# An attention and feed-forward kernel: the planner that orders its instructions makes eight passes with deadlines, and the Softplus of four banks is planned as two operations of two

## The chip, the cores and the metric

The kernel runs on one core of a Trainium2 chip. A core has several engines that work side by side, each on its own queue of instructions, in the order in which the program lists them: TensorE (PE, matrix products; PEld is its weight load), VectorE (DVE), ScalarE (ACT), GpSimd (POOL), and SyncE (SP), which here issues all DMAs. An instruction waits until the semaphores of what it needs have been raised, and everything behind it on the same engine waits with it. The metric is the device time of one execution in microseconds (us), as the median of several runs.

## The reference

What is computed, cut to what matters (float32; the feed-forward weights arrive as float64):

```python
# attention: B=8, H=8, S=576, D=64, keys and values averaged over groups of 8
k_p = k.reshape(B, H, 72, 8, D).mean(axis=3)
v_p = v.reshape(B, H, 72, 8, D).mean(axis=3)
attn = softmax(1/sqrt(D) * q @ k_p.transpose(0, 1, 3, 2))
x = (attn @ v_p).transpose(0, 2, 1, 3).reshape(4608, 512)
# feed-forward: 512 -> 2048 -> 512
h = x @ w_in
g = h * erf(log(1 + exp(h)))
return g @ w_out
```

## The kernel before

**Tiling.** The 4608 tokens are cut into nine chunks of 512, with tokens along the free axis and features on the 128 partitions. Attention goes block by block (at most 256 tokens of one batch, `job`, lines 456 to 638): loads of keys and values that DVE sums over groups of eight (`ks<-raw`, `vs<-v`, line 470), scores on PE (`att<-kbd,q`, line 520), a maximum, a subtraction, an exponential by way of Sigmoid and a sum, a transpose on PE (lines 572 and 575), and the product with the values (lines 615 and 616), whose result is copied out of PSUM as a part of `x`. Each factor of a large product is split into a high and a low part (`halves`, lines 340, 341 and 352), and three matmuls of 512 columns stand for one product (`three`, line 687).

**Stages.** Chunk 0 is done plainly: `plain_in` (16 first-layer tiles in groups of four) and `second` (the second layer). The weights are unpacked from float64 on the way (lines 386 to 399), used, and stored to HBM for later (lines 409, 412, 420, 422). Chunks 1 to 8 go in four pairs. For each pair the first layer is a scheme of seven products instead of eight (`sides`, `head`, `quad`: eight quads of four output tiles each). Some of its weights are sums of weight blocks, called `ws` (`sums`, line 430 to 444); the first pair makes them on the fly. The second layer of the first pair is plain, that of the other pairs again takes seven products (`seconds`). The activation of each group of four tiles (`activation`, line 689) is Softplus on four banks of PSUM or four tiles (`d<-h` or `d<-g`, line 697), Erf on the two 1024-wide halves (`d<-d`, line 701), and a multiplication with `h` on DVE or POOL (`g<-d,h`, line 708, and `g<-d,g`, line 705). Softplus and Erf (which shares a table set with the Sigmoid of the attention) need different tables on ACT, so a table load stands where the kind changes.

**What sets the order.** None of this is written in the order in which it runs. Every call of `op` (line 143) notes an operation: its engine or two engines to choose from, a cost in ns, a priority `prio` (a due time written out by hand, in units of some 5 us), and the buffers that it reads and writes. `order` (line 182) is a list scheduler: it keeps the time at which each engine is free, looks at the operations that are ready, and on each engine picks the one with the least start time plus 30 ns (400 ns on SP) for each unit of `prio`; then it takes the earliest of the engines' picks. Buffers are places: there are 87 places of 2 KB for all large tiles, eight banks of PSUM, and a limit for each kind of tile (`CAPS`, line 52; `h` may hold 6 banks). An operation whose first touch of a tile finds no free place starts when one comes free. `WINDOW` keeps an operation from running more than 10 units ahead. A change of the ACT tables is planned at 1300 ns. Before the first large product PE is kept busy with filler matmuls on constants (`h<-cst`, line 937); the planner puts in as many as its idle time there holds (line 246).

Of the kernel before, what the change touches and what calls it, by code (L numbers as in the profile page):

```python
# [13 lines left out]
AF = mybir.ActivationFunctionType  # L14
# [7 lines left out]
SP = S // POOL  # L22
# [14 lines left out]


WINDOW = 10
T0, T0_STEP = -10.5, 1.5  # L40
VAL_R = 3.5
KEYS, KEYS_R, KEYS_S = -5.5, 0.5, -1.0
# [13 lines left out]
DGE = 1200  # L56
# [71 lines left out]
class Program:  # L128
# [14 lines left out]
    def op(self, eng, cost, prio, fn, reads=(), writes=(), hold=(), alt=None, funcs=None, port=False, turn=None):  # L143


        o = Op(eng, cost, prio, fn)
        o.set, o.port = funcs, port
        o.choice = {eng: (cost, fn)}
        if alt:
            o.choice[alt[0]] = alt[1:]  # L150
        o.bufs.extend(hold)
        deps = {}
        for accesses, write in ((reads, False), (writes, True)):
            for a in accesses:
                buf, key = a if isinstance(a, tuple) else (a, None)
                if isinstance(buf, Buf) and buf not in o.bufs:
                    o.bufs.append(buf)
                for k, (writer, readers) in buf.state.items():
                    if key is None or k is None or k == key:
                        for d in ([writer] if writer else []) + (readers if write else []):  # L160
                            if d is not o:
                                deps[d] = deps.get(d, False) or d is writer
                if write:
                    if key is None:
                        buf.state.clear()
                    buf.state[key] = (o, [])
                else:
                    buf.state.setdefault(key, (None, []))[1].append(o)
        for b in o.bufs:
            b.left += 1  # L170
        for d, flow in deps.items():
            d.next.append((o, flow))
            o.wait += 1
        if turn is not None:
            if turn in self.turns:
                self.turns[turn].follow.append(o)
                o.wait += 1
            self.turns[turn] = o
        self.ops.append(o)
        return o  # L180

    def order(self):
        free = {e: 0.0 for e in self.DELAY}
        free["SP"] = 2150.0
        port = 0.0
        slots = {t: [(0.0, i) for i in range(n)] for t, n in self.capacity.items()}
        avail = {e: [] for e in free}
        for i, o in enumerate(self.ops):
            o.key = (o.prio, i)
# [6 lines left out]
        spare = None  # L196
# [3 lines left out]
        for _ in self.ops:  # L200
# [38 lines left out]
            loaded = o.set or loaded  # L239
            if spare is not None and o.eng == "PE":  # L240
                if start > FILL:
                    heapq.heappush(slots["bank"], (start, spare[1]))
                    spare = None
                else:
                    idle = start - max(free["PE"], 3000.0) - MARGIN - (1800 if not free["PE"] else 0)
                    out.extend([self.filler] * int(idle / 107))
            end = free[o.eng] = start + o.cost
            if e == "POOL" or (e == "DVE" and o.port):
                port = end
            o.done = True  # L250
            while todo and todo[0][2].done:
                heapq.heappop(todo)
            progress = todo[0][0] if todo else progress
            for b in o.bufs:
                if not b.held:
                    b.held = True
                    b.places = {t: heapq.heappop(slots[t])[1] for t in b.limits}
                    b.place = b.places[b.home]
                b.left -= 1
                b.end = max(getattr(b, "end", 0.0), end)  # L260
                if not b.left:
                    for t in b.limits:
                        heapq.heappush(slots[t], (b.end + 150, b.places[t]))
            for d in o.follow:
                d.wait -= 1
                if not d.wait:
# [26 lines left out]
def moe_attention(ctx: ExitStack, tc: tile.TileContext, cst, qa, kl, vl, wi, wo, out):  # L293
    nc = tc.nc
# [26 lines left out]
    def act(n, psum=False):  # L321
        return 0.84 * n + (160 if psum else 190)
# [366 lines left out]
    def activation(hs, prio):  # L689

        ys = [Buf(space, [P, 2, 512], F32, "d", "d") for _ in range(2)]
        y = lambda k: ys[k // 2].ap[:, k % 2]
        own = [(ys[k // 2], k % 2) for k in range(4)]

        def softplus():
            for k, (h, _) in enumerate(hs):
                nc.scalar.activation(y(k), h.ap, AF.Softplus)  # L697

        op("ACT", 4 * act(512), prio, softplus, [h for h, _ in hs], own, funcs="softplus")
        for k in range(2):  # L700
            op("ACT", act(1024), prio + 0.2, lambda k=k: nc.scalar.activation(ys[k].ap, ys[k].ap, AF.Erf),  # L701
               own[2 * k:2 * k + 2], own[2 * k:2 * k + 2], funcs="sigmoid")
        for k, (h, g) in enumerate(hs):
            if g is h:
                both(True, dve(512), gps(512), prio + 0.3, lambda e, k=k, h=h: e.tensor_mul(  # L705
                    h.ap, y(k), h.ap), [own[k], h], [h])
            else:
                op("DVE", dve(512), prio + 0.3, lambda k=k, h=h, g=g: nc.vector.tensor_mul(  # L708
                    g.ap, y(k), h.ap), [own[k], h], [g])
# [270 lines left out]
```

## Time and profile before

| | |
|---|---|
| median of 3 runs | 883.96 us (883.89 to 884.6) |
| the profiled execution | 884.53 us |
| its span, first to last instruction | 882.5 us |
| mean granted TensorE clock in it | 0.992 |
| DVE busy | 713.5 us (81%) |
| POOL busy | 437.9 us (50%) |
| matmuls of line 687 (512 columns each) | 1584 + 1344 + 192 |
| DMA | 218.03 MB, 72.2% of what 16 DMA engines' time would hold |

A row of instructions reads: line, engine, operation, tile written `<-` tiles read, shape, count `x`; after the bar the busy time and the mean ns of one, then idle time of the engine ahead of them and what ended it. In a timeline a row begins with its start and its length in us, and the bracket at its end is the idle time ahead of it and what released it. In a table of windows each engine has its busy us in that stretch; PEclk is the granted TensorE clock, DMA the mean busy share of the DMA engines.

### The profile page before, as it was taken

The page shows a single profiled execution, that of the slowest core. Times are in us where ns is not written, and L with a number is a line of the kernel's source. Part 1 is how long each engine was busy: PE and PEld are TensorE (multiplying, and loading weights), DVE is VectorE, ACT ScalarE, POOL GpSimd, SP SyncE. Part 2 cuts the span into 40 slices and gives each one's busy share as a digit, 9 for nine tenths or more (in the row PEclk, how much of TensorE's full clock was granted, in tenths as well). Part 3 has the DMA queues.
Part 4 walks back from the last instruction along what each step waited for, and adds up shares of the span by engine and source line. Part 5 has one row for each costly group of instructions (what it writes and reads, how often), then busy time and mean ns, then how long its engine had stood idle before and what let it go on. Part 6 is the DMA issues. An engine that isn't in the chain of part 4 may idle for free. (4 is left out here: it accounts for less than half of the span.)

```text
span 882.5 us, 13579 instructions
## 1 busy us (share of the span) xinstructions
PE 852.9 (97%) x4106; PEld 701.0 (79%) x4106; DVE 713.5 (81%) x1264; ACT 561.6 (64%) x1002; POOL 437.9 (50%) x453
## 2 busy tenths in 40 slices
PE   8989899979899999999999999999999999999998
PEld 6777788768778888888887888888888888888886
DVE  5978779868888889578999998889898984567982
ACT  4778867648964475268766734587867445887630
POOL 1777578436856883035485333155474312484210
PEclk9999999989999999999999999999999999999999
DMA  8677999799898959997474367974633679448541
GB/s 286 228 243 243 295 353 321 253 375 383 294 340 315 374 196 375 353 355 268 141 267 146 119 204 262 352 238 121 227 120 120 203 268 350 118 121 266 175 163 52
DMA packets 125207, 218.03 MB, mean 247 GB/s; under 512 B 16976, under 2 KB 31440, under 8 KB 125136
## 3 DMA queue, kind: packets, MB, share of 16 engines
q1 hardware_dynamic: 125136, 217.18, 72.2%
q8 instruction: 33, 0.54, 0.3%
q14 instruction: 38, 0.31, 0.1%
HBM read 167.84 MB, written 49.28 MB: 246 GB/s over the span
## 5 line engine op out<-in xcount | busy, mean ns | idle before, releaser
L687 PE MATMUL o<-gl,w 128*128 128x512 f32 x1584 | 377.0, 393 | 1.6 <-DVE gl L352 1.4
L687 PEld LDWEIGHTS o<-gl,w 128*128 128x128 f32 x1584 | 292.7, 188 | 63.5 <-DVE gl L352 1.8
L687 PE MATMUL h<-x,w 128*128 128x512 f32 x1344 | 319.1, 394 | 7.5 <-DVE g L708 3.0
L687 PEld LDWEIGHTS h<-x,w 128*128 128x128 f32 x1344 | 250.9, 189 | 62.1 <-DVE g L708 3.2
L340 ACT ACTIVATE gl<-g 128x512 fp32r<-128x512 f32 x204 | 119.7, 624 | 74.9 <-DVE g L833 32.0
L352 POOL TENSOR_TENSOR gl<-g,gl 128x512 fp32r<-128x512 f32 x77 | 108.1, 1410 | 66.8 <-ACT gl L340 62.3
L705 POOL TENSOR_TENSOR g<-d,g 128x512 f32<-128x512 f32 x54 | 69.8, 1310 | 107.6 <-ACT d L701 93.8
L352 DVE TENSOR_TENSOR gl<-g,gl 128x512 fp32r<-128x512 f32 x139 | 107.6, 807 | 0.4 <-ACT gl L340 0.2
L770 DVE TENSOR_TENSOR g<-t,h 128x512 f32<-128x512 f32 x96 | 65.6, 684 | 41.0 <-PE h L687 39.9
L701 ACT ACTIVATE d<-d 128x1024 f32<-128x1024 f32 x72 | 72.7, 1051 | 0.3
L833 POOL TENSOR_TENSOR g<-g 128x512 f32<-128x512 f32 x48 | 67.3, 1413 | 8.8 <-DVE gl L352 6.1
L697 ACT ACTIVATE d<-g 128x512 f32<-128x512 f32 x103 | 57.5, 622 | 5.3 <-DVE g L770 5.2
L770 DVE TENSOR_TENSOR t<-t,h 128x512 f32<-128x512 f32 x57 | 39.1, 686 | 24.1 <-PE h L687 22.7
L687 PE MATMUL h<-x,ws 128*128 128x512 f32 x192 | 49.0, 410 | 6.8 <-DVE x L352 4.5
L561 POOL TENSOR_TENSOR bb<-s,z 128x64 f32<-128x64 f32 (+1 forms) x40 | 12.9, 322 | 81.1 <-DVE z L555 26.6
L687 PEld LDWEIGHTS h<-x,ws 128*128 128x128 f32 x192 | 38.1, 200 | 16.5 <-issue 6.3
L340 ACT ACTIVATE x<-xr 128x512 fp32r<-128x512 f32 (+2 forms) x64 | 34.4, 559 | 25.1 <-DVE xr L661 12.0
L615 PE MATMUL att<-et,va 128*128 128x256 f32 (+3 forms) x192 | 46.1, 340 | 1.4 <-DVE g L708 0.6
L520 PE MATMUL att<-kbd,q 128*128 128x144 f32 (+1 forms) x320 | 46.3, 287 | 1.2 <-issue 0.7
L520 PEld LDWEIGHTS att<-kbd,q 128*128 128x128 f32 (+1 forms) x320 | 42.2, 179 | 6.1 <-issue 2.2
L697 ACT ACT_TABLE_LOAD x36 | 46.2, 1283 | 0.6
L549 ACT ACTIVATE s<-s,cst 128x576 f32<-128x576 f32 (+1 forms) x36 | 27.9, 775 | 25.0 <-DVE s L545 24.8
(92 smaller groups left out, 1153.4 us busy)
## 6 DMA issues: line engine op xcount, KB each, us to landing
w<-ws SPq DMA_DIRECT2D x192, 256.0 KB, 4.8
w<-wo SPq DMA_DIRECT2D x136, 256.0 KB, 3.8
w<-wi SPq DMA_DIRECT2D x96, 256.0 KB, 5.0
ws<-ws SPq DMA_DIRECT2D x64, 256.0 KB, 5.3
v<-vl SPq DMA_DIRECT2D x48, 256.0 KB, 5.3
raw<-kl SPq DMA_DIRECT2D x32, 288.0 KB, 4.3
out<-f SPq DMA_DIRECT2D x36, 256.0 KB, 2.1
q<-qa SPq DMA_DIRECT2D x32, 256.0 KB, 5.1
```

The costliest lines, as they stand in the source:

```text
L340: op("ACT", act(n), prio, lambda: nc.scalar.activation(dst(), src(), AF.Copy, scale=scale), *access, turn=turn, alt=("POOL", 0.833 * n + 1 ...
L352: both(True, dve(n), gps(n), prio + 0.1, lambda e: e.tensor_sub(lo(), src(), f32(hi())), reads + [hikey], [lokey])
L520: nc.tensor.matmul(o, raw.ap[:, p, :T], kbd[:, p], start=(p % 2 == 0), stop=True, skip_group_check=True)
L549: op("ACT", act(H * SP) + 93, r + 0.8, lambda: nc.scalar.activation(s.ap[:T], s.ap[:T], AF.Sigmoid, bias=bias[0][:T], scale=1.0 / 64.0), [ ...
L561: nc.gpsimd.tensor_mul(bb.ap[:T], sv, zv.unsqueeze(2).broadcast_to([T, NP, 16]))
L615: nc.tensor.matmul(o, va[:, p], et.ap[:, p, :n], start=e == 0, stop=False, skip_group_check=True)
L687: nc.tensor.matmul(o, u, v, start=first and q == 0, stop=last and q == 2, skip_group_check=True)
L697: nc.scalar.activation(y(k), h.ap, AF.Softplus)
L701: op("ACT", act(1024), prio + 0.2, lambda k=k: nc.scalar.activation(ys[k].ap, ys[k].ap, AF.Erf), own[2 * k:2 * k + 2], own[2 * k:2 * k + 2 ...
L705: both(True, dve(512), gps(512), prio + 0.3, lambda e, k=k, h=h: e.tensor_mul(h.ap, y(k), h.ap), [own[k], h], [h])
L770: op("DVE", dve(512), prio, lambda: nc.vector.tensor_add(dst.ap, u.ap, o.ap), [u, o], [dst])
L833: both(True, dve(512), gps(512), prio, lambda e: e.tensor_sub(out.ap, u.ap, v.ap), [u, v], [out])
```

## The change

The planner's one run becomes the function `once`, and `order` calls it up to eight times. After each pass `latest` goes through the operations from the last to the first and works out the latest time at which each may start without making that pass longer: from the operations that need its result, from the operation that followed it on its engine, and, through the new list `after`, from the operation that took over its place in memory. These times, divided by 5100, replace `prio` in the next pass. Of all passes the one with the least planned length is kept. In the program as built all eight passes run, and the fourth is the one kept. In `activation` the Softplus of four banks, one operation until now, becomes two operations of two, which the planner may place apart. Line numbers behind 182 grow, by 59 up to `three` and by 61 from `activation` on: 470 is now 529, 687 is 746, 697 is 758, 701 is 762, 708 is 769.

```diff
@@ the planner
+PASSES, UNIT = 8, 5100.0
...
-    def order(self):
+    def reset(self):
...
+    def latest(self):
+        for o in self.ops:
+            o.late = self.length
+        for o in sorted(self.ops, key=lambda o: -o.start):
+            at = o.late - o.cost
+            for d, flow in o.next:
+                gap = self.DELAY[o.eng] if d.eng != o.eng else (self.SAME[o.eng] if flow else 0)
+                at = min(at, d.late_at - gap - o.cost)
+            for d, gap in o.after:
+                at = min(at, d.late_at - gap - o.cost)
+            o.late_at = at
+
+    def order(self, passes=PASSES):
+        best = None
+        self.prios = [o.prio for o in self.ops]
+        for n in range(passes):
+            self.reset()
+            try:
+                out = self.once()
+            except RuntimeError:
+                break
+            if best is None or self.length < best[0]:
+                best = (self.length, out, [(o.eng, o.cost, o.fn, o.start) for o in self.ops],
+                        [(b, b.place) for o in self.ops for b in o.bufs])
+            self.latest()
+            for o, p in zip(self.ops, self.prios):
+                o.prio = o.late_at / UNIT
+        self.length, out, how, places = best
...
+    def once(self):
...
+            if o.eng in last:
+                last[o.eng].after.append((o, 0))
+            last[o.eng] = o
...
-                    b.places = {t: heapq.heappop(slots[t])[1] for t in b.limits}
+                    b.places = {}
+                    for t in b.limits:
+                        _, b.places[t], by = heapq.heappop(slots[t])
+                        if by is not None and by is not o:
+                            by.after.append((o, 150 + (DGE if e == "SP" else 0)))
...
@@ the activation
-        def softplus():
-            for k, (h, _) in enumerate(hs):
-                nc.scalar.activation(y(k), h.ap, AF.Softplus)
-
-        op("ACT", 4 * act(512), prio, softplus, [h for h, _ in hs], own, funcs="softplus")
+        for i in (0, 2):
+
+            def softplus(i=i):
+                for k in (i, i + 1):
+                    nc.scalar.activation(y(k), hs[k][0].ap, AF.Softplus)
+
+            op("ACT", 2 * act(512), prio + 0.01 * i, softplus, [h for h, _ in hs[i:i + 2]], own[i:i + 2], funcs="softplus")
```

No instruction of the mathematics is added or removed. What the new order changes in kind and number: ACT holds 97 table loads instead of 73 (6 more in the stage of chunk 0, and 6, 8, 4 and 0 in the quads of the four pairs); the fillers on PE are 206 instead of 178; of the operations with a choice of engine some change sides (multiplications `g<-d,g` on POOL 68 instead of 54, high halves `gl<-g` on ACT 185 instead of 204, among others); SP issues the same 807 instructions.

**ACT, the first group of Softplus.** These are the first Softplus (`d<-h`, straight from the banks of PSUM) of chunk 0, with the Erf behind them (`d<-d`); `cv`, `low` and `w` are steps of unpacking weights. Before:

```order
L389 ACTIVATE cv<-d 128x512
L697 ACT_TABLE_LOAD
L697 ACTIVATE d<-h 128x512 x4
L389 ACTIVATE cv<-d 128x512
L701 ACT_TABLE_LOAD
L701 ACTIVATE d<-d 128x1024 x2
L340 ACTIVATE gl<-g 128x512
```

and in the changed kernel:

```order
L758 ACT_TABLE_LOAD
L758 ACTIVATE d<-h 128x512 x2
L448 ACTIVATE cv<-d 128x512
L452 ACTIVATE low<-d,cst 128x512
L762 ACT_TABLE_LOAD
L762 ACTIVATE d<-d 128x1024
L758 ACT_TABLE_LOAD
L758 ACTIVATE d<-h 128x512 x2
L448 ACTIVATE cv<-d 128x512
L762 ACT_TABLE_LOAD
L762 ACTIVATE d<-d 128x1024
```

Two banks now go through Softplus and Erf before the next two are begun, with two more table loads for the four.

**DVE, the multiplications that free those banks.** `g<-d,h` reads a bank of `h` for the last time; `vs<-v` and `ks<-raw` are sums over values and keys that come by DMA. Before:

```order
L397 SCALAR_TENSOR_TENSOR cv<-cv,low 128x512
L399 SCALAR_TENSOR_TENSOR f_934<-d,cv 128x512
L470 TENSOR_REDUCE vs<-v 128x64
L708 TENSOR_TENSOR g<-d,h 128x512 x4
L397 SCALAR_TENSOR_TENSOR cv<-cv,low 128x512 x2
```

and in the changed kernel:

```order
L458 SCALAR_TENSOR_TENSOR f_963<-d,cv 128x512
L612 TENSOR_SCALAR z<-z 64x8
L529 TENSOR_REDUCE ks<-raw 128x72
L769 TENSOR_TENSOR g<-d,h 128x512 x2
L614 RECIPROCAL z<-z 64x8
L411 TENSOR_TENSOR gl<-g,gl 128x512
L456 SCALAR_TENSOR_TENSOR cv<-cv,low 128x512
L458 SCALAR_TENSOR_TENSOR f_1039<-d,cv 128x512
L769 TENSOR_TENSOR g<-d,h 128x512 x2
```

The four multiplications stood together behind a sum over values; now they stand in two pairs, the first behind a sum over keys.

**PE, the way into the first products with `ws`.** These are the last products with the values for chunks 1 and 2 (`att<-et,va` and `att<-etb,vb`), the first-layer products with stored weights (`h<-x,w`), and the first products with sums of weights (`h<-x,ws`), which need all of `x` of both chunks. Before:

```order
L616 MATMUL att<-etb,vb 64x128
L687 MATMUL h<-x,w 128x512 x24
L615 MATMUL att<-et,va 128x128
L616 MATMUL att<-etb,vb 64x128
L615 MATMUL att<-et,va 128x128
L616 MATMUL att<-etb,vb 64x128
L687 MATMUL h<-x,ws 128x512 x18
L687 MATMUL h<-x,w 128x512 x12
```

and in the changed kernel:

```order
L675 MATMUL att<-etb,vb 64x128
L746 MATMUL o<-gl,w_2023 128x512 x2
L746 MATMUL o<-gl,w_2223 128x512
L746 MATMUL h<-x,w 128x512 x12
L674 MATMUL att<-et,va 128x128
L675 MATMUL att<-etb,vb 64x128
L674 MATMUL att<-et,va 128x128
L675 MATMUL att<-etb,vb 64x128
L746 MATMUL h<-x,ws 128x512 x18
L746 MATMUL h<-x,w 128x512 x12
```

In both the products with `ws` follow the last product with the values directly, with no other product between them.

More of the change, by code (lines that the diff above doesn't have):

```diff
@@ L180, in op @@
         return o
-    def order(self):
+    def reset(self):
+        for o in self.ops:
+            if not hasattr(o, "first"):
+                o.first = (o.wait, o.eng, o.cost, o.fn)
+            o.wait, o.eng, o.cost, o.fn = o.first
+            o.ready, o.done, o.before = 0.0, False, []
+            for b in o.bufs:
+                b.left, b.held, b.end, b.last = 0, False, 0.0, None
+        for o in self.ops:
+            for b in o.bufs:
+                b.left += 1
+    def latest(self):
+        for o in self.ops:
+            o.late = self.length
[23 more added lines that the diff above has]
+        self.length, out, how, places = best
+        for o, h in zip(self.ops, how):
+            o.eng, o.cost, o.fn, o.start = h
+        for b, p in places:
+            b.place = p
+        return out
+    def once(self):
+        for o in self.ops:
+            o.after = []
+        last, porter = {}, None
         free = {e: 0.0 for e in self.DELAY}
@@ L185, in order @@
         port = 0.0
-        slots = {t: [(0.0, i) for i in range(n)] for t, n in self.capacity.items()}
+        slots = {t: [(0.0, i, None) for i in range(n)] for t, n in self.capacity.items()}
         avail = {e: [] for e in free}
@@ L241, in order @@
                 if start > FILL:
-                    heapq.heappush(slots["bank"], (start, spare[1]))
+                    heapq.heappush(slots["bank"], (start, spare[1], None))
                     spare = None
@@ L256, in order @@
                     b.held = True
-                    b.places = {t: heapq.heappop(slots[t])[1] for t in b.limits}
+                    b.places = {}
[3 more added lines that the diff above has]
+                            by.after.append((o, 150 + (DGE if e == "SP" else 0)))
                     b.place = b.places[b.home]
                 b.left -= 1
-                b.end = max(getattr(b, "end", 0.0), end)
+                if end >= b.end:
+                    b.end, b.last = end, o
                 if not b.left:
                     for t in b.limits:
-                        heapq.heappush(slots[t], (b.end + 150, b.places[t]))
+                        heapq.heappush(slots[t], (b.end + 150, b.places[t], b.last))
             for d in o.follow:
```

## The prediction

> **What bounds the kernel now.** I read the page first, its busy shares and its slices.
>
> ```profile
> span 882.5 us, 13579 instructions
> PE 852.9 (97%) x4106; PEld 701.0 (79%) x4106; DVE 713.5 (81%) x1264; ACT 561.6 (64%) x1002; POOL 437.9 (50%) x453
> PE   8989899979899999999999999999999999999998
> L340 ACT ACTIVATE gl<-g 128x512 fp32r<-128x512 f32 x204 | 119.7, 624 | 74.9 <-DVE g L833 32.0
> L697 ACT ACT_TABLE_LOAD x36 | 46.2, 1283 | 0.6
> ```
>
> PE is the bound: from the 13th slice on (about 260 us) it is at nine tenths nearly throughout. No matmul of the mathematics goes away, so the change can only win time in which PE stands still or runs at a lower clock. Next the table of windows, for PE alone (columns: PE busy, granted clock, DMA share, GB/s):
>
> ```profile
> 40.00:60.00 20.00, 18.25 (x89) 1.00 0.66 214
> 60.00:80.00 20.00, 18.43 (x74) 0.91 0.82 265
> 80.00:100.00 20.00, 18.68 (x88) 1.00 0.85 261
> 100.00:120.00 20.00, 17.58 (x91) 1.00 1.02 355
> 120.00:140.00 20.00, 20.00 (x110) 1.00 0.98 328
> 140.00:160.00 20.00, 18.74 (x98) 1.00 0.90 302
> 160.00:180.00 20.00, 15.45 (x75) 0.96 0.78 261
> 180.00:200.00 20.00, 18.81 (x74) 0.87 1.06 383
> 220.00:240.00 20.00, 17.69 (x72) 0.91 0.82 300
> 240.00:260.00 20.00, 18.65 (x86) 1.00 0.97 323
> 460.00:480.00 20.00, 18.62 (x93) 1.00 0.57 201
> ```
>
> Idle time is 20 less the busy time. Between 40 and 200 us it adds to 14.1 us, in 220 to 260 to 3.7, and one stall of 1.4 stands at 471. The clock takes more: 9% of 20 us at 60 to 80 (1.8 us), 4% and 13% at 160 to 200 (3.4), 9% at 220 to 240 (1.8). That is 26.2 us in all, and only 1.4 of it lies behind 260 us. The timeline of PE names the stalls:
>
> ```profile
> 61.24 10.06 PE L687 MATMUL h<-x,w 128*128 128x512 f32 x36 [2.99 <-DVE g L708]
> 71.63 2.97 PE L687 MATMUL h<-x,w 128*128 128x512 f32 x12 [0.33 <-DVE s L545]
> 85.36 3.00 PE L687 MATMUL h<-x,w 128*128 128x512 f32 x12 [1.00 <-DVE s L545]
> 176.16 0.50 PE L687 MATMUL h<-x,ws 128*128 128x512 f32 x1 [0.96 <-ACT x L340]
> 180.99 1.62 PE L687 MATMUL h<-x,ws 128*128 128x512 f32 x3 [4.32 <-DVE x L352]
> 231.87 2.00 PE L687 MATMUL h<-x,w 128*128 128x512 f32 x6 [2.31 <-DVE t L770]
> 244.64 1.62 PE L687 MATMUL h<-x,ws 128*128 128x512 f32 x6 [1.35 <-DVE g L770]
> 473.02 4.19 PE L687 MATMUL o<-gl,w 128*128 128x512 f32 x17 [1.38 <-DVE gl L352]
> ```
>
> The three long ones (2.99, 4.32, 2.31) are each followed by a low clock in the windows. The Trainium skill ("TensorE: Matmul & The Clock Gate", Part 1) lets the clock fall to half after an idle window of about 3.4 us. Here 2.99 and 2.31 were enough. By the page those two clock losses would not belong to the stalls, and the sum below would be smaller by at most 2.7 us; the rows decide.
>
> The full pace of the large matmuls stands in the chain of work that ended last, 204 in 46.26 us or 227 ns each:
>
> ```profile
> 679.80 46.26 PE o L687 x204
> ```
>
> **Part 1: banks of h in chunk 0 (40 to 100 us).** Six banks may hold h, so the seventh product waits until a bank has been through Softplus, Erf and the multiplication. ACT and DVE there:
>
> ```profile
> 49.78 1.28 ACT L697 ACT_TABLE_LOAD   x1
> 51.08 2.06 ACT L697 ACTIVATE d<-h 128x512 f32<-128x512 f32 x4
> 53.69 1.28 ACT L701 ACT_TABLE_LOAD   x1
> 54.98 2.01 ACT L701 ACTIVATE d<-d 128x1024 f32<-128x1024 f32 x2
> 59.90 0.69 DVE L470 TENSOR_REDUCE vs<-v 128x64 f32<-128x512 f32 x1 [3.08 <-DMA v<-vl]
> 60.51 1.87 DVE L708 TENSOR_TENSOR g<-d,h 128x512 f32<-128x512 f32 x3
> ```
>
> Erf was done at 56.99, but the multiplication stood behind a sum over values that waited 3.08 us for its DMA. Now the first two banks go through ACT alone, and need not wait for the third and fourth. A bank of products takes 12 matmuls, 2.7 us at 227 ns, so the pair can start up to 5.4 us sooner. That covers the 3.08, should the sum over keys that now stands ahead of the pair wait as long. The rows at 71.63 and 85.36 name a DVE step, but what they want is again a bank. I cost all three as gone: 2.99 + 0.33 + 1.00 and the 1.8 of clock, **6.1 us**; bounds 0 (DVE's new neighbour waits longer than 5.4) and 6.4 (all idle time of 40 to 100 us and the clock).
>
> **Part 2: 100 to 160 us.** The 3.7 us idle here are short waits in the attention of chunks 1 and 2. The order shows no single one that must go. Counted in the order in which the program is written out: from the first large product to the first with `ws`, 34 groups of matmuls stood directly behind the last step of another engine that they need (no other group between that step's start and theirs); now 13 do. I take half, **1.9 us**, between 0 and 3.7.
>
> **Part 3: the first products with ws (160 to 200 us).** The order puts nothing between the last values and these products, before as after, so a chain of copies, subtractions and splits stays exposed. But part of the stall is something else:
>
> ```profile
> 177.45 0.55 DVE L352 TENSOR_TENSOR x<-xr,x 128x384 fp32r<-128x384 f32 x1
> 180.08 0.96 DVE L352 TENSOR_TENSOR x<-xr,x 128x384 fp32r<-128x384 f32 x3 [2.07 <-DMA wf<-f]
> 181.99 1.17 DVE L352 TENSOR_TENSOR x<-xr,x 128x384 fp32r<-128x384 f32 x4 [0.75 <-ACT x L340]
> wf<-f SPq DMA_DIRECT2D x32, 256.0 KB, 4.6
> ```
>
> DVE waits 2.07 us for a store (`wf<-f`): the new tile of x takes the place of a weight tile whose store, 4.6 us from issue to landing, has not landed. In the planner's places, 25 of 185 places left by a store are taken again within six SP instructions (8 within three, five of those by tiles of x). After the change it is none of 158, since `latest` now counts a place as a dependence. I take both waits as gone, 2.07 + 0.75 = 2.8, and with the stall cut to about 1.5 to 2 us one of the two stretches of low clock, half of 3.4: **4.5 us**, between 0 and 9.1 (5.7 idle and 3.4).
>
> **Part 4: the first quads, and the rest.** At 231.87 and 244.64 PE waits for DVE's additions out of the banks; 3.7 us and 1.8 of clock. The order changes ACT most here (part 5), so I take half, **2.7 us**, between 0 and 5.5. Of the 1.4 at 473, half: **0.7**.
>
> **Part 5: what is added.** The fillers grow from 178 to 206.
>
> ```profile
> 14.34 3.98 PE L937 MATMUL h<-cst 128*128 128x256 bf16 x35
> ```
>
> At 3.98/35 = 0.114 us the 28 more take **3.2 us**, all ahead of the first large product. If they only cover time in which PE would wait for data anyway they cost nothing (bound 0); I take 3.2, since the planner leaves PE no earlier work. 24 more table loads of 1.283 us are 30.8 us of ACT, whose share of 64% would become 67%; the 19 high halves `gl<-g` that leave ACT give back 11.9 at 624 ns. I cost the loads at nothing, because PE's work in those stretches hides them, with rival B for the case that it doesn't.
>
> **Sum:** 6.1 + 1.9 + 4.5 + 2.7 + 0.7 - 3.2 = 12.7 us. Profiled execution 884.53 (span 882.5 and 2.0 around it) - 12.7 = 871.8; the median of the runs lies 0.6 under that execution, so **871.2 us**.
>
> **Rival A: DMA takes the gain back.** In the order written out, 191 SP instructions stand ahead of the first product with ws, not 169: 22 of 256 KB, 5.6 MB, which at the 383 GB/s of the fullest window above take 14.7 us. From 100 to 160 us the DMA engines are at 0.90 to 1.02 already. If these transfers must land first, that product comes no sooner than before, and parts 1 to 3 and the 3.2 cancel; only part 4 is left, 3.4 us: 884.0 - 3.4 = 880.6. Against it: many of the 22 are stores that nothing there reads.
>
> **Rival B, slower: ACT becomes the bound in the first quads.** Windows with all engines (PE, PEld, DVE, ACT, POOL):
>
> ```profile
> 200.00:220.00 20.00, 20.00 (x90) 16.57 (x89) 15.80 (x25) 18.09 (x26) 14.68 (x15) 1.00 1.05 381
> 220.00:240.00 20.00, 17.69 (x72) 14.14 (x71) 16.39 (x29) 19.10 (x29) 17.82 (x20) 0.91 0.82 300
> 240.00:262.00 22.00, 20.65 (x95) 16.82 (x93) 19.15 (x29) 16.33 (x20) 10.50 (x11) 1.00 0.97 331
> ```
>
> ACT is busy 53.5 of 62 us here, 19.1 of 20 in the middle. The first pair's eight quads get 6 more loads, 7.7 us; some 6.0 us of these fall into the 62, 59.5 in all. It decides where waits of ACT's own use up the 2.5 us that are left: then the loads push the multiplications, the banks and PE, and cost 7.7, part 4 wins nothing, and against them and the 3.2 only part 1 remains: 884.0 + 7.7 + 3.2 - 6.1 = 888.8. For it: the stalls at 232 and 244 lie exactly there. Against it: ACT gives up high halves in exchange, and the planner reckons with 1300 ns for a load, where the row shows 1283. The Trainium skill ("ScalarE: Activation LUTs", What ACT_TABLE_LOAD costs) speaks against the change more strongly: about 1.28 us for the load and about 1.38 more to drain, 2.66 for each switch. The rows of part 1 show the load at 49.78 ended by 51.06 and Softplus begun at 51.08, with no such gap; by the page's price 6 loads would bring these 62 us to 69.5, and rival B would hold.
>
> **Rival C: the stalls only move.** The planner's durations aren't the chip's, and it ranks by its own. If on the chip as much is lost elsewhere as is saved, the time stays: 884.
>
> **Chances.** Forecast 0.63 (864 to 878). Rival A 0.15 (880.6), rival B 0.13 (888.8), rival C 0.09. A measurement of this kernel can tell 0.2% (1.8 us) from no change. Faster: forecast and A, 0.78; same: C, 0.09; slower: B, 0.13. The range: below, all idle time and low clock gone, against the fillers, 884.0 - 26.2 + 3.2 = 861; above, to the old time, 884, which takes in A and half of C and leaves out B.
>
> **What would show it.** Part 1: no PE stall over 1 us between the first large product and 90 us, and a clock of 1.00 at 60 to 80. Part 2: fewer short waits at `att`. Part 3: the first product with ws some 5 us ahead of 176, less than 3 us of idle time at it, and no wait of DVE for `wf<-f` there. Part 4: an ACT share under 95% in the first quads and shorter waits for `t` and `g`. Part 5: the first large product 3 us later. Wrong it would be if PE waits for DMA ahead of the ws products (A), if ACT's busy time fills the first quads and PE waits there for 5 us or more (B), or if idle time appears behind 260 us, where PE had next to none.

## The result, and the profile after

The changed kernel takes **870.23 us** (median of four runs, 869.22 to 872.59) against 884.28 for the kernel before on the same chip (883.89 to 885.38): the ratio is 0.9843, with a 95% interval from 0.9821 to 0.9865. The profiled execution took 870.09 us. The forecast was 871.2, in a range from 861 to 884.

From the page of the changed kernel: the span, the engines' busy time, and the table loads of ACT ahead of Softplus (behind the bar busy time and mean ns; then idle time ahead of them and what ended it).

```profile
span 868.3 us, 13644 instructions
PE 850.9 (98%) x4134; PEld 702.7 (81%) x4134; DVE 698.6 (80%) x1272; ACT 574.4 (66%) x989; POOL 459.9 (53%) x482
L758 ACT ACT_TABLE_LOAD x48 | 61.6, 1283 | 20.7 <-PE h L746 20.0
```

ACT took on the table loads at the predicted price. Ahead of those for Softplus it now waits 20.7 us, 20.0 of them by the profile for matmuls into `h`; before it was 0.6. So ACT often stands ready before PE has filled a bank.

Where the time went is read from PE's timeline, at the first large product, at the first and the last group with `ws`, and at the last group of all. The kernel before (its first `ws` product, at 176.16, stands in the prediction):

```profile
40.67 16.61 PE L687 MATMUL h<-x,w 128*128 128x512 f32 x72
255.62 1.52 PE L687 MATMUL h<-x,ws 128*128 128x512 f32 x6
874.81 3.56 PE L687 MATMUL o<-gl,w 128*128 128x512 f32 x15
```

The changed kernel, with the waits that are left in between:

```profile
44.48 27.46 PE L746 MATMUL h<-x,w 128*128 128x512 f32 x120
72.88 13.91 PE L746 MATMUL h<-x,w 128*128 128x512 f32 x60 [0.76 <-DVE g L769]
92.71 0.41 PE L674 MATMUL att<-et,va 128*128 128x64 f32 x2 [1.41 <-DVE s L604]
...
170.63 0.47 PE L746 MATMUL h<-x,ws 128*128 128x512 f32 x1 [2.88 <-POOL sw L496]
172.72 6.95 PE L746 MATMUL h<-x,ws 128*128 128x512 f32 x17 [1.62 <-DVE x L411]
...
214.86 1.66 PE L746 MATMUL h<-x,w 128*128 128x512 f32 x6 [0.68 <-DVE t L831]
...
244.19 1.52 PE L746 MATMUL h<-x,ws 128*128 128x512 f32 x6
...
861.74 2.65 PE L746 MATMUL o<-gl,w 128*128 128x512 f32 x11
```

| stage, us | before | after | difference |
|---|---|---|---|
| to the first large product | 40.67 | 44.48 | +3.8 |
| from there to the first `ws` | 135.49 | 126.15 | -9.3 |
| from there to the last group with `ws` | 79.46 | 73.56 | -5.9 |
| from there to PE's end | 622.75 | 620.20 | -2.6 |
| behind PE's end, to the end of the span | 4.1 | 3.9 | -0.2 |

The differences add to the -14.2 by which the span shrank. Most of it, 11.4 us, lies ahead of 245 us, where PE used to wait. The same stretches in the table of windows (PE, PEld, DVE, ACT, POOL; clock, DMA share, GB/s), first the kernel before, then the changed one:

```profile
40.00:100.00 60.00, 55.36 (x250) 44.84 (x248) 47.05 (x87) 45.82 (x67) 40.82 (x47) 0.97 0.78 247
100.00:160.00 60.00, 56.32 (x296) 45.69 (x295) 52.41 (x109) 42.88 (x93) 44.96 (x54) 1.00 0.97 328
160.00:200.00 40.00, 34.25 (x149) 27.18 (x148) 30.10 (x65) 21.43 (x48) 16.08 (x21) 0.91 0.92 322
200.00:260.00 60.00, 56.34 (x244) 46.03 (x243) 49.56 (x79) 52.73 (x72) 41.01 (x41) 0.97 0.95 335
```

```profile
40.00:100.00 60.00, 57.57 (x285) 47.48 (x284) 47.81 (x91) 53.39 (x76) 45.98 (x54) 1.00 0.95 321
100.00:160.00 60.00, 60.00 (x313) 49.66 (x312) 54.58 (x110) 44.85 (x95) 49.14 (x56) 1.00 1.00 360
160.00:200.00 40.00, 35.31 (x148) 28.43 (x147) 35.82 (x71) 27.03 (x49) 26.27 (x30) 0.91 0.94 335
200.00:260.00 60.00, 58.99 (x265) 48.04 (x264) 53.54 (x87) 53.31 (x68) 47.60 (x54) 1.00 0.87 292
```

The length less PE's busy time is idle, and the part of the clock below 1.00 is lost as well. From 40 to 100 us that was 4.64 + 1.8 and is 2.43; from 100 to 160 it was 3.68 and is nothing; from 200 to 260 it was 3.66 + 1.8 and is 1.01. Only the third row stands nearly still, 5.75 + 3.6 against 4.69 + 3.6: a stall at the first `ws` products is there as before, and so is a stretch of low clock.

### The profile page after: what moved, and what is told of

Its sections match the earlier page's. It is cut to its first block, busy times and chain, and to the rows that moved or that the text cites. A ratio compares the mean times of both kernels' runs of the same rounds, so it can differ in the third digit from the quotient of the medians.

```text
span 868.3 us, 13644 instructions
## 1 busy us (share of the span) xinstructions
PE 850.9 (98%) x4134; PEld 702.7 (81%) x4134; DVE 698.6 (80%) x1272; ACT 574.4 (66%) x989; POOL 459.9 (53%) x482
## 4 chain that ended last, share of the span: by engine, by line
PE 72%; DVE 2%; issue 0%; ACT 0%; DVEq 0%
PE o L746 36%; PE h L746 29%; PE att L579 3%; PE att L674 3%; PE att L631 1%; PE att L675 1%; DVE g L766 0%; DVE gl L411 0%; PE att L634 0%; DVE g L894 0%; DVE g L831 0%; DVE f L918 0%; DVE ks L529 0%; DVE t L831 0%; DVE s L624 0%
## 5 line engine op out<-in xcount | busy, mean ns | idle before, releaser
L766 POOL TENSOR_TENSOR g<-d,g 128x512 f32<-128x512 f32 x68 | 90.7, 1351 | 98.7 <-ACT d L762 75.8
L399 ACT ACTIVATE gl<-g 128x512 fp32r<-128x512 f32 x185 | 109.3, 625 | 46.2 <-DVE g L894 20.2
L411 POOL TENSOR_TENSOR gl<-g,gl 128x512 fp32r<-128x512 f32 x67 | 100.0, 1501 | 66.8 <-ACT gl L399 32.4
L411 DVE TENSOR_TENSOR gl<-g,gl 128x512 fp32r<-128x512 f32 x149 | 110.2, 767 | 6.2 <-POOL gl L400 3.9
L758 ACT ACT_TABLE_LOAD x48 | 61.6, 1283 | 20.7 <-PE h L746 20.0
L894 POOL TENSOR_TENSOR g<-g 128x512 f32<-128x512 f32 x36 | 51.8, 1439 | 25.0 <-DVE g L894 19.3
L399 ACT ACTIVATE x<-xr 128x512 fp32r<-128x512 f32 (+2 forms) x60 | 32.5, 563 | 28.9 <-DVE xr L720 21.5
L642 ACT COPY et<-att 128x512 f32<-128x512 f32 (+1 forms) x40 | 21.8, 544 | 34.5 <-PE att L631 33.5
```

Source lines behind the costliest of these rows:

```text
L399: op("ACT", act(n), prio, lambda: nc.scalar.activation(dst(), src(), AF.Copy, scale=scale), *access, turn=turn, alt=("POOL", 0.833 * n + 1 ...
L411: both(True, dve(n), gps(n), prio + 0.1, lambda e: e.tensor_sub(lo(), src(), f32(hi())), reads + [hikey], [lokey])
L642: op("ACT", act(4 * T, True), r + 2.3, lambda: nc.scalar.copy(et.ap[:, :, cs], pav()), [pa], [(et, k)])
L758: nc.scalar.activation(y(k), hs[k][0].ap, AF.Softplus)
L894: both(True, dve(512), gps(512), prio, lambda e: e.tensor_sub(out.ap, u.ap, v.ap), [u, v], [out])
```

## The experiments

Three questions were open. Which part of the change does it, the deadlines or the split Softplus? Does the time follow the length that the planner itself works out (874.0 us for the order before, 859.5 for the pass kept), plus a fixed rest of some ten us? And what holds the stall at the first `ws` products? Planned lengths below are the planner's own.

**One part alone.** First the split Softplus with a single pass, ranked by the due times written by hand:

```diff
-PASSES, UNIT = 8, 5100.0
+PASSES, UNIT = 1, 5100.0
```

> One pass with the hand-written priorities, Softplus in two of two. The planner's own planned length for this order is 871.4 us (874.0 for the kernel before, 859.5 for the changed one). Theory 1 (the gain is the planner's: a plan carries over to the chip with a nearly constant excess, 10.2 us for the kernel before and 10.8 for the changed one): about 881.9 us, so nearly all of the gain is lost. Theory 2 (the split is what frees the banks of h, part 1 of the prediction): the stall at 61 us and its low clock go, 6 us are won, about 878, with no PE wait over 1 us between the first large product and 90 us.

Measured: 880.95 us (seven runs, 879.75 to 882.41), ratio 0.9961 [0.9943, 0.998]: a gain of 3.4 us, between the two forecasts and nearer to that of theory 1. PE's timeline shows the stall at 61 us gone, as theory 2 has it, 132 matmuls in one run from the first large product on. That time is lost again at two later places. By the windows PE is idle for 3.88 us from 80 to 100 us, with a clock of 0.91 (before: 1.32 us and 1.00), and for 6.66 us from 160 to 200, with a clock of 0.83 (before: 5.75 us and 0.91). The second place is the first `ws` products:

```profile
40.49 30.21 PE L746 MATMUL h<-x,w 128*128 128x512 f32 x132
...
174.93 4.21 PE L746 MATMUL h<-x,ws 128*128 128x512 f32 x9 [2.97 <-DVE x L411]
181.87 3.78 PE L746 MATMUL h<-x,ws 128*128 128x512 f32 x8 [2.73 <-DVE x L411]
```

The view of the waits from 100 to 200 us (engine, line, waited for: us in all, times, longest) says what stood behind them:

```profile
POOL x L400 <- DMA wf<-f: 12.0, 1, 12.0
ACT x L399 <- DMA wf<-f: 5.0, 1, 5.0
```

Without the deadlines tiles of `x` still take places whose store has not landed; here it is ACT and POOL that wait for it.

Then eight passes with the Softplus of four in one operation:

```diff
-        for i in (0, 2):
-
-            def softplus(i=i):
-                for k in (i, i + 1):
-                    nc.scalar.activation(y(k), hs[k][0].ap, AF.Softplus)
-
-            op("ACT", 2 * act(512), prio + 0.01 * i, softplus, [h for h, _ in hs[i:i + 2]], own[i:i + 2], funcs="softplus")
+        def softplus():
+            for k, (h, _) in enumerate(hs):
+                nc.scalar.activation(y(k), h.ap, AF.Softplus)
+
+        op("ACT", 4 * act(512), prio, softplus, [h for h, _ in hs], own, funcs="softplus")
```

> Eight passes with deadlines, Softplus of four banks in one operation; the second pass is kept, planned length 867.5 us. Theory 1: about 878.0 us, that is under half of the gain, since the passes need the split to find the better order. Theory 2 (parts 2 to 4 of the prediction come from the deadlines, part 1 from the split): the waits for banks of h ahead of 90 us stay at some 4 us with a low clock after them, the rest is won: about 876.

Measured: 869.57 us (868.31 to 870.61), ratio 0.983 [0.9811, 0.985]; both theories gave a time too long. The deadlines alone give all of the gain, and the split adds nothing to it that can be measured. From PE's timeline:

```profile
70.93 13.85 PE L746 MATMUL h<-x,w 128*128 128x512 f32 x60 [2.49 <-DVE f L458]
...
170.72 0.49 PE L746 MATMUL h<-x,ws 128*128 128x512 f32 x1 [1.47 <-ACT x L399]
172.79 5.67 PE L746 MATMUL h<-x,ws 128*128 128x512 f32 x17 [1.57 <-DVE x L411]
```

It keeps a stall of 2.49 us where the changed kernel has 0.76. That wait ends with `f<-d,cv`, a step of unpacking weights, and not with the multiplication that frees a bank of `h`, so it does not show what the split does; the kernel with the split alone does that. Its waits at the `ws` products are 1.5 us shorter (1.47 + 1.57 against 2.88 + 1.62). It has 73 table loads, the changed kernel 97, and the times are equal within the spread: the 24 loads cost nothing that shows.

**The dependence through places.** `latest` without the places that an operation takes over:

```diff
                         _, b.places[t], by = heapq.heappop(slots[t])
-                        if by is not None and by is not o:
-                            by.after.append((o, 150 + (DGE if e == "SP" else 0)))
```

> As the changed kernel, but the deadlines don't count the taking over of a place in memory as a dependence; planned length 864.2 us, third pass kept. Theory 1: about 874.7 us. Theory 2 (part 3: the place dependence keeps tiles of x off places whose store has not landed): DVE waits for a store of weights again ahead of the first product with ws, and some 4.5 us are lost against the changed kernel: also about 874.7, but with that wait in the trace. In this order no place left by a store is taken again within three SP instructions (6 within six), so theory 1 expects no such wait.

Measured: 870.43 us (869.08 to 872.28), ratio 0.9842 [0.9821, 0.9863], the same as with them, and 4 us under what both theories gave. The waits from 100 to 200 us have no entry for a store `wf<-f` here either. So the places need not be counted to get rid of those waits. The kernel before and the one with the split alone, both ranked by hand, have them; none of the twelve profiled kernels with deadlines has them in that stretch.

**Another pass.** The last of the eight orders instead of the shortest (planned 868.1 instead of 859.5):

```diff
-            if best is None or self.length < best[0]:
+            if best is None or n == passes - 1:
```

> As the changed kernel, but the eighth pass is kept instead of the fourth; planned length 868.1 us instead of 859.5. Theory 1: about 878.7 us. Rival (the planner's lengths differ by less than its errors, so that any pass with deadlines does as well): within 2 us of the changed kernel, 868 to 872.

Measured: 872.97 us (872.62 to 874.35), ratio 0.9874 [0.9853, 0.9895]: 2.7 us above the changed kernel, where the plans differ by 8.6. That is 1 us above the rival's range and 5.7 under theory 1. Two passes only, planned 863.8:

```diff
-PASSES, UNIT = 8, 5100.0
+PASSES, UNIT = 2, 5100.0
```

> As the changed kernel with two passes instead of eight; the second is kept, planned length 863.8 us (859.5 with eight). Theory 5 (any order by deadlines wins about the same; what the planner gains below some 868 is lost on the chip to durations that it doesn't know): 868 to 873. Rival (planned gains carry over): 4.3 us slower than the changed kernel, 874.5.

Measured: 875.15 us, but the four runs lie from 871.22 to 880.1 and the interval from 0.984 to 0.995, so this one decides nothing.

**Half the fillers.**

```diff
-                    out.extend([self.filler] * int(idle / 107))
+                    out.extend([self.filler] * int(idle / 214))
```

> As the changed kernel, with 100 fillers instead of 206 and nothing else moved. 106 fillers at 0.109 us are 11.6 us of PE time ahead of the first large product, which stands at 44.5 us (40.7 before the change). Theory 3 (the fillers only cover waits; the later first product comes from the chain of chunk 0's attention): the first large product stays within 0.7 us of 44.5 and the total within 1 us of 870.2. Rival (part 5 of the prediction: the fillers themselves are the price): it comes 3 us or more sooner, and some of that reaches the end.

Measured: 873.92 us (870.75 to 878.73), ratio 0.9896 [0.9847, 0.9946]. Two of the four runs are near 871 us and two at 877 and 879, so what the fillers do to the total stays undecided. The profiled execution took 870.75. With 106 fillers fewer its first large product begins at 44.14, against 44.48:

```profile
36.89 0.30 PE L634 MATMUL att<-cst,bb 128*64 128x128 f32 x1 [3.09 <-POOL bb L620]
...
44.14 16.15 PE L746 MATMUL h<-x,w 128*128 128x512 f32 x70
```

PE just stands where the fillers were. They do not make the product late; it waits for `x` of chunk 0. The next rows follow the attention that makes the second half of that `x`, first in the changed kernel, then in the kernel before: DVE's reciprocal (`z<-z`), what POOL does ahead of its next step `bb`, and PE's product with `bb`.

```profile
34.84 0.19 DVE L614 RECIPROCAL z<-z 128x8 f32<-128x8 f32 x1
35.09 1.27 POOL L411 TENSOR_TENSOR w<-f,w 128x512 fp32r<-128x512 f32 x1
36.67 0.30 PE L634 MATMUL att<-cst,bb 128*64 128x128 f32 x1 [0.73 <-POOL bb L620]
```

```profile
32.74 0.20 DVE L555 RECIPROCAL z<-z 128x8 f32<-128x8 f32 x1
33.54 0.30 PE L575 MATMUL att<-cst,bb 128*64 128x128 f32 x1 [1.10 <-POOL bb L561]
```

The `bb` product ahead of this one stands at 29.8 us in both, so the delay arises here: of the 3.8 us, 3.1 are there at this product. The new order has DVE sum values (`vs<-v`, L529) and do more of the unpacking ahead of the reciprocal, which comes 2.1 us later, and has POOL finish a low part of weights before `bb`. The last 0.7 come behind it, where DVE begins the softmax of the next block (L588 and L604) before the last parts of `x`; that this takes them is read from the order.

**Cover for the stall.** The last 12 first-layer products (two heads) are moved behind the last products with the values, and two copies with them:

```diff
     ops = pr.order()
+    named = lambda o, n: o.eng == "PE" and o.fn.__name__ == n
+    ws = next(i for i, o in enumerate(ops) if named(o, "go") and o.bufs[0].name == "ws")
+    vs = [i for i in range(ws) if named(ops[i], "values")][-2:]
+    heads = [ops[i] for i in range(vs[0]) if named(ops[i], "go")][-2:]
...
+    ops = rest(0, vs[1] + 1) + heads + rest(vs[1] + 1, ws) + copies + rest(ws, len(ops))
```

> As the changed kernel, but two first-layer products (12 matmuls, 2.7 us) stand behind the last products with the values instead of ahead of them, so that they cover the chain into the first product with ws; the two copies out of their banks move with them. The changed kernel loses 4.5 us of idle time and 3.4 of clock there. Theory 4 (what is left of that stall is the exposed chain from the values to x): 2 to 3 us less idle time there, and one or both stretches of low clock gone, total 866 to 868. Rival (DVE and POOL set the time of that product by the amount of their work, not by the chain): the first product with ws stays at 170.6 or later and the total at 870.

Measured: 872.03 us (870.67 to 874.39), ratio 0.9859 [0.9831, 0.9888]. PE's timeline:

```profile
167.27 2.96 PE L746 MATMUL h<-x,w 128*128 128x512 f32 x12
172.51 0.54 PE L746 MATMUL h<-x,ws 128*128 128x512 f32 x1 [2.28 <-POOL sw L496]
```

2.9 us of work now lies between the last values and the `ws` product, and the wait is still 2.28 us, as the rival has it. In this execution PE was already 2.4 us later at the second-layer products ahead of the edit (165.21 against 162.82, with a clock of 0.91 from 60 to 80 us). Counted from there, the products with the values come some 2.9 us sooner than in the changed kernel, the `ws` product only 0.5. What holds it is not the distance from the values: DVE is still making the `ws` and the `x` that it reads.

**Durations nearer to the chip's.** The Softplus of four in one operation, POOL planned at 2.65 ns a column instead of 2.33, DVE's additions and the like (`both`) 10% dearer, up to twelve passes:

```diff
-PASSES, UNIT = 8, 5100.0
+PASSES, UNIT = 12, 5100.0
...
-        return 2.33 * n + 110
+        return 2.65 * n + 110
...
-        op("DVE", cost, prio, lambda: fn(nc.vector), *access, port=True,
+        op("DVE", 1.1 * cost, prio, lambda: fn(nc.vector), *access, port=True,
```

> Eight passes become twelve, Softplus of four in one operation, and the planner's costs are brought nearer to the trace: POOL 2.65 instead of 2.33 ns for an element (1467 ns for 512, where the trace of the changed kernel has 1351 to 1501), DVE operations that share work with POOL 10% longer (761, trace 767). Theory 5: a plan that knows these durations loses less on the chip: 864 to 868. Rival (the remaining loss isn't due to these durations): 869 to 873 as the other kernels with deadlines.

Measured: 878.26 us (876.74 to 879.21), ratio 0.9925 [0.9899, 0.9952]: slower than with the planner's own numbers by 8.7 us against the passes alone. Built again, this kernel's planner makes only four passes, since in the fifth it comes to a point at which no operation can go on, and keeps the fourth, 880.0 us long by its new costs. These mark-ups did not make a better plan.

**POOL beside DVE at the stall.** In the changed kernel, rows of DVE, POOL and ACT ahead of the first `ws` products:

```profile
168.17 1.81 DVE L411 TENSOR_TENSOR ws<-sw,ws 128x256 fp32r<-128x256 f32 x2
169.91 2.09 DVE L720 TENSOR_TENSOR xr<-xr 128x128 f32<-128x128 f32 x6
171.92 0.95 DVE L411 TENSOR_TENSOR x<-xr,x 128x384 fp32r<-128x384 f32 x3
```

```profile
167.97 0.87 POOL L495 TENSOR_TENSOR sw<-sw 128x256 f32<-128x256 f32 x1
168.91 0.79 POOL L496 TENSOR_TENSOR sw<-sw 128x256 f32<-128x256 f32 x1
```

```profile
170.22 0.31 ACT L399 ACTIVATE x<-xr 128x128 fp32r<-128x128 f32 x1 [1.52 <-DVE xr L720]
```

PE's row names `sw` of POOL as what released the first `ws` product at 170.63, but that sum was done at 169.70. What ends 0.1 us ahead of the product is this high part of `x` on ACT (170.53), which waited 1.52 us for a sum `xr` that stood in DVE's queue behind two low parts of `ws`. Those two take DVE 1.81 us while POOL adds other `sw`. The next run gives those two sums to DVE, at the place in the program that they have now:

```diff
     ops = pr.order()
+    ws = next(i for i, o in enumerate(ops) if o.eng == "PE" and o.fn.__name__ == "go" and o.bufs[0].name == "ws")
+    for o in [o for o in ops[ws:] if o.eng == "POOL" and o.bufs and all(b.name == "sw" for b in o.bufs)][:2]:
+        o.fn = o.choice["DVE"][1]
```

> As the changed kernel, but the two sums (128x256) that POOL runs at 168 to 170 us, while DVE makes the last parts of the first product with ws, go to DVE's queue behind those parts; all else stays. In the changed kernel DVE's two low halves (128x256) at 168.2 take 1.81 us together, where such an operation alone takes 0.42. Theory 6 (POOL and DVE slow each other when both work in SBUF): the two low halves take about 0.85 together, and the first product with ws comes about 1 us sooner (169.6 instead of 170.6). Rival (DVE waits for something else there, such as the values): the two take 1.8 us as before.

Measured: one run, 867.36 us. DVE's timeline and PE's:

```profile
168.39 0.75 DVE L411 TENSOR_TENSOR ws<-sw,ws 128x256 fp32r<-128x256 f32 x2
```

```profile
169.79 0.47 PE L746 MATMUL h<-x,ws 128*128 128x512 f32 x1 [1.81 <-issue]
```

The pair takes 0.75 us in place of 1.81, and the product begins 0.8 us earlier. The kernel with both edits, below, has the sums on DVE too, and the pair takes 0.76 us in its profile. One run says nothing of so little in the whole time.

**Fillers that keep the clock up.** Filler matmuls on constants ahead of the first `ws` product, 26 of them in the changed kernel and 18 in the one with the passes alone:

```diff
+            if w.name == "ws" and not lead:
+                lead.append(w)
+                for _ in range(26):
+                    nc.tensor.matmul(o.ap[:, :256], cb[:, :P], cb[:, :256], start=True, stop=True)
```

> As the changed kernel, with 26 fillers (2.8 us) on PE directly ahead of the first product with ws, written into its own bank, where PE stands idle for 2.9 us and then runs at half clock for 6.8 us. Theory 7 (the idle time of the stall is what lowers the clock): one or both stretches of low clock go, the total is 867 to 869. Rival (the low clock follows from the second gap of 1.6 us alone, or from something other than idle time): the clock stays low there, the total is 870 or more.

> As e2 (eight passes, Softplus of four banks in one), with 18 fillers (2.0 us) ahead of the first product with ws. e2 has one stretch of low clock of 3.4 us there, after 1.5 and 1.6 us of idle time. Theory 7: that stretch goes, 1.7 us are won, 867 to 868.5. Rival: 869.6 as e2.

Measured: 871.13 us (866.89 to 875.78), ratio 0.9858 [0.9809, 0.9907], and 869.38 us (867.88 to 871.07), ratio 0.9836 [0.9796, 0.9876]. Both totals are nearer to what the rival gave, 870 or more and 869.6. In the profiled execution of the first, 866.89, PE's timeline reads:

```profile
166.04 3.01 PE L801 MATMUL h<-cst 128*128 128x256 bf16 x26
169.12 0.47 PE L746 MATMUL h<-x,ws 128*128 128x512 f32 x1
171.69 4.18 PE L746 MATMUL h<-x,ws 128*128 128x512 f32 x17 [2.11 <-DVE x L411]
```

The 17 products take 4.18 us where they took 6.95, so the clock stays up and 2.8 us are won there. In the second they take 4.56 us where they took 5.67, and the window from 160 to 180 us is at 1.00 where it was at 0.91. So theory 7 is right about the clock at this place. The medians do not show it: other runs of the first kernel are up to 8.9 us above that execution. One reason is to be seen in the second, at a place far ahead of its edit:

```profile
70.72 15.44 PE L746 MATMUL h<-x,w 128*128 128x512 f32 x60 [2.46 <-ACT d L756]
```

The kernel with the passes alone has the same order there, and its row at 70.93 above shows the same 60 matmuls behind a wait of 2.49 us in 13.85 us. The clock from 60 to 80 us was 1.00 there and 0.91 here. So the same stall in the same order is followed by a low clock in one execution and not in another, and that is 1.6 us.

**Both together**, the sums on DVE as above and 22 fillers:

```diff
+    for o in [o for o in ops[ws:] if o.eng == "POOL" and o.bufs and all(b.name == "sw" for b in o.bufs)][:2]:
+        o.fn = o.choice["DVE"][1]
...
+                for _ in range(22):
+                    nc.tensor.matmul(o.ap[:, :256], cb[:, :P], cb[:, :256], start=True, stop=True)
```

> As the changed kernel with both edits: the two sums of 168 us on DVE behind the chain (e9, in whose one look the first product with ws came 0.8 us sooner and the total was 867.4) and 22 fillers ahead of that product (e10, whose profile had no low clock there, 3.4 us, at 866.9). If both readings hold and add, the first product with ws stands at 169 to 170 us, the clock is full there and the total is 864 to 867 against 870.2 for the changed kernel. If they are one effect (e10's sooner product already in it), 866 to 869.

Measured: 871.49 us (869.95 to 872.31), ratio 0.9843 [0.9816, 0.987]. This missed. The gain at the first products is there, and it is lost again at other places, by PE's timeline and the windows of PE alone:

```profile
173.56 4.19 PE L746 MATMUL h<-x,ws 128*128 128x512 f32 x17 [1.25 <-DVE x L411]
...
188.29 1.66 PE L746 MATMUL h<-x,w 128*128 128x512 f32 x6 [1.02 <-DVE t L837]
...
250.26 0.70 PE L579 MATMUL att<-kbd,q 128*64 128x144 f32 x4 [2.02 <-DVE g L837]
```

```profile
80.00:100.00 20.00, 18.18 (x92) 0.91 0.96 319
...
240.00:260.00 20.00, 16.91 (x74) 0.91 0.75 273
```

The window from 80 to 100 us lies ahead of the edit and yet shows a low clock that the changed kernel's own profile does not have (1.00 there): part of this is spread between executions. None of the versions is clearly faster than the changed kernel.

**The planned length** answers the second question. Measured less planned is 10.3 us for the kernel before and 10.7 for the changed one, which looks like a fixed rest; but it is 9.5 for the split alone (planned 871.4), 2.1 for the passes alone (867.5), 6.2 without place dependences (864.2) and 4.9 for the eighth pass. The theory of a constant falls. These orders with deadlines, planned from 859.5 to 868.1, all end between 869.6 and 873.0 (the undecided two passes aside). The order worked out with other costs (878.26 us) stands outside this: not every order with deadlines does as well.

## Why the prediction was right, point by point

The time and its sign were right, and so was the mechanism: PE's idle time and low clock, nearly all of it ahead of 260 us. That the sum came within 1 us is in part luck, since its terms miss in both directions: the banks of `h` were put 2.1 us and the `ws` products 3.4 us too high, 100 to 160 us 1.8, the first quads 1.8 and the rest 1.3 too low. One term had the right size for a wrong reason.

- **Banks of h (6.1 predicted).** In 40 to 100 us 6.4 was lost and now 2.4, 4.0 won. The 2.99 and its low clock are gone as said, and a wait of 1.41 for `s` stands at 92.71. The prediction counted the waits of 0.33 and 1.00 for `s` as waits for a bank that the split frees; by their rows they end with `s<-att,m`, a read of scores, which the split does not touch. The split alone removes the stall at 61 us too, but it is not what made the kernel faster: without deadlines most of the time reappears from 80 to 100 us and at the `ws` products, and with deadlines the kernel with the Softplus of four is as fast.
- **100 to 160 us (1.9).** All 3.7 are gone; PE is busy 60.00 of 60.00. Taking half was too careful.
- **First products with `ws` (4.5).** This step failed. It said that the waits for the store would go, which they did: the changed kernel has no wait of DVE or ACT for `wf<-f` from 100 to 200 us. But the places counted in `latest` are not needed for it, as the run without them shows, and the time did not come back: 9.4 us were lost in 160 to 200 and 8.3 still are, 1.1 won. In place of the wait for the store stands a wait for DVE's own queue, made longer by POOL beside it, and its 2.88 + 1.62 us are again followed by a low clock. The prediction named less than 3 us of idle time there as the sign that the step holds; it is 4.50.
- **First quads (2.7) and the rest (0.7).** 4.5 us were won in 200 to 260, and some 2.0 of idle time behind that, where the prediction counted 1.4 in all and PE's timeline of the kernel before has 2.25. Both halves taken were too careful.
- **Fillers (3.2).** The first large product is 3.8 us later, the size predicted, but the cause was wrong: half the fillers give back only 0.3. What goes with it is the attention of chunk 0, which stands behind sums over values and unpacking on DVE and POOL. That these cause it was read from the two orders and not tried by itself.
- **The table loads (0).** Right; 24 more or fewer make no difference that shows, though the two orders compared differ in other things too.

Rival B, with ACT as the bound in the first quads, is refuted by the window of the changed kernel over the last 62 us of the stage with `ws` (same columns as above):

```profile
183.00:245.00 62.00, 60.79 (x266) 49.37 (x265) 54.41 (x83) 56.42 (x68) 48.64 (x57) 1.00 0.90 303
```

ACT is busy 56.42 of 62 us, 91%, and PE hardly waits at all. The prediction's 69.5 us puts all six loads into this stretch, where its sum by the rows puts 6.0 of 7.7 us there; by that share it would be 66 us. Rival A, with DMA taking back the gain, falls as well: the DMA engines did fill up (0.95 and 1.00 in the first two windows, where they had 0.78 and 0.97), but the first `ws` product came 5.5 us sooner, and the wait ahead of it ends with work of DVE and ACT. Rival C was right in one stage only, the first `ws` products.

Between the first large product and PE's end 17.8 us were won. By the windows above, 3.6 of them are the clock (two rows at 0.97 are now at 1.00, 1.8 each) and 9.6 idle time of PE from 40 to 260 us (17.7 before, 8.1 now); behind that PE's timeline has some 2.0 us less idle (2.25 before, 0.21 now). The 2.6 that remain lie in the lengths of the matmul rows themselves, and I can't place them; they are less than the 3.4 us by which the four runs of the changed kernel differ. Two things stay open: why orders whose plans differ by 8 us end within about three, and where the gains of single edits at the `ws` stall go from run to run. A clock that falls behind one and the same stall in some executions only is part of the second, 1.6 us at the place shown; that it is all of it is not shown.

The prediction took from the rows that waits of 2.99 and 2.31 us are enough for a low clock. In those rows they were; the wait of 2.49 us in the kernel with the passes alone was not.

## What to carry to other kernels

When a list scheduler runs on due times written by hand, let it work out deadlines from its own plan before any operation is cut finer: here that gave the whole gain, while the finer cut alone gave 0.4% and moved most of the stall to later places. Do not read the planner's length as a forecast: plans from 859.5 to 868.1 us came within 3.4 us of each other on the chip. And test each cause alone even when the time came out as forecast: here one term had the right size for a wrong reason, and a wait that went as forecast left its place to another.

## What the runs showed of the hardware

- DVE subtractions with two operands in SBUF, 128x256, took 0.75 and 0.76 us for two with no POOL operation beside them, and 1.81 us for two while POOL made sums in SBUF. The Trainium skill ("GPSIMD Engine Reference", 1. Specifications) says that POOL's interfaces to SBUF are shared with VectorE and contend with DVE instructions that have two inputs there; these rows agree, and give the size for this shape.
- After a wait of 1.47 and one of 1.57 us with a single matmul between them, the clock was lowered: 17 products took 5.67 us in place of 4.18. With fillers just ahead, a gap of 2.11 us was followed by the full pace.
- The length of a gap alone does not decide it. In two executions with the same order of instructions up to there, 60 matmuls took 13.85 us behind a gap of 2.49 us and 15.44 us behind one of 2.46.
